# Longformer attention followed by a squared-ReLU feed-forward: inputs through hardware DMA queues with a GpSimd cast, 120-row tiles, a shared PSUM ring and a reordered start

## The chip, the cores and the metric

The kernel runs on one core of one Trainium2 chip. The metric is the device time of one execution in microseconds (us); several executions are timed and their median is given. All runs quoted here count as fast: none took over 1.5% more than the fastest of the same kernel. "PE" is TensorE, "DVE" VectorE, "ACT" ScalarE, "POOL" GpSimd, "SP" the sync engine, which here only issues DMAs. SBUF and PSUM are the on-chip memories; matmul results land in PSUM. A "casting" DMA changes fp32 to fp16 on the way.

## The reference, cut to what matters

```python
def _attn_ref(q, k, v, global_idx):          # q, k, v: (8, 8, 576, 64) float32
    scores = (1 / sqrt(64)) * q @ k.T
    mask = (abs(i - j) <= 32) | is_global[i] | is_global[j]   # 8 global positions
    attn = softmax(where(mask, scores, -1e9))
    return attn @ v

def _moe_ref(x, w_in, w_out):                # x: 4608 x 512, w_in: 512 x 2048, w_out: 2048 x 512
    r = maximum(x @ w_in, 0)
    return (r * r) @ w_out
```

Eight batches of eight heads each give 4,608 tokens of 512 features. The feed-forward (called "expert" below) works on nine chunks of 512 tokens. A chunk can start when the batches that hold its tokens are done.

## The kernel before

The 576 keys of a head lie in five tiles of 116, 116, 116, 116 and 112 rows, with 8 global rows behind them. All inputs come through casting DMAs issued by GpSimd:

```python
KT = 116
KN = (116, 116, 116, 116, 112)
...
    def load_k(b):                            # load_q, load_v alike
        t = knat[b % 2]                       # [128, 5, 512] fp16
        for i in range(NT):
            nc.gpsimd.dma_start(
                out=t[0 : KN[i], i].rearrange("p (h d) -> p h d", d=D),
                in_=k[b, :, KT * i : KT * i + KN[i], :].rearrange("h s d -> s h d"),
            )
        # the global rows follow from a scratch in DRAM, through SP
```

One such DMA moves 116 x 8 runs of 64 numbers. The expert part uses PSUM through two separate tags, two buffers for `ph` and one for `po`:

```python
    def mm1(c, u):
        ph = ps.tile([P, TC], FP32, name="ph", tag="m1", bufs=2)
        ...                                   # 4 matmuls of 512 columns
        nc.scalar.activation(out=rl, in_=ph, func=AF.Relu)
        nc.vector.tensor_tensor(out=gts[c][:, u, :], in0=rl, in1=rl, op=ALU.mult)

    def mm2(c, m, part, tag="m2", bufs=1):
        if part == 0:
            po_now[0] = ps.tile([P, dm], FP32, name="po", tag=tag, bufs=bufs)
        ...                                   # 4 matmuls; after part 3:
            nc.vector.tensor_copy(out=ot, in_=po)      # then a store through SP
```

The main loop has 64 slots, one per head. A slot emits the scores of its head, one transpose for a later head, up to four expert units ("fills", taken from chunk 0 at slot 10, chunk 1 at slot 18 and so on), and the product with v ("PV") of the head before:

```python
    for s in range(B * H):
        b, h = divmod(s, H)
        ...                                   # gathers of global rows at h == 2
        if h == 1 and b >= 1 and b + 1 < B: load_v(b + 1)
        if h == 6 and b + 2 < B: load_k(b + 2); load_q(b + 2)
        et = scores(b, h)
        ...                                   # nb, nhp: a later head pair
        (tr_q if h % 2 == 0 else tr_k)(nb, nhp)
        fill(s, 2)
        if prev is not None: pv(*prev)
        fill(s, 2)
        prev = (b, h, et)
```

The last PV of a batch also copies eight global columns into `xT` on GpSimd (`xT <- gx`), and the expert units of the next chunk wait for that copy. What is left of the fills follows after the loop.

The softmax here doesn't subtract the row's maximum and nothing guards it: scores larger than these inputs give would overflow.

Of the kernel before, what the change touches and what calls it, by code (L numbers as in the profile page):

```python
# [18 lines left out]
KT = 116  # L19
NT = 5  # L20
KN = (116, 116, 116, 116, 112)
# [3 lines left out]
NCOL = 600  # L25

WIN = (
    (0, 0, 0, 0, 156),
    (1, 0, 156, 84, 188),
    (2, 0, 344, 208, 96),  # L30
    (2, 1, 0, 304, 100),
    (3, 1, 100, 332, 188),
    (4, 1, 288, 448, 152),
# [6 lines left out]
def kernel(  # L40
# [37 lines left out]
    for i in range(2):  # L78
        nc.sync.dma_start(
            out=gq64[64 * i : 64 * i + 64],  # L80
            in_=gsrc.to_broadcast((NG, H)).unsqueeze(2),
        )
    gp64 = sbt("gp64", [P, 1], I64)
    nc.vector.memset(gp64.bitcast(I32), 0)
    nc.sync.dma_start(out=gp64[KT : KT + NG, :], in_=gsrc)
    g64 = sbt("g64", [1, NG], I64)
    nc.sync.dma_start(out=g64, in_=global_idx.unsqueeze(0))

# [3 lines left out]
    nc.gpsimd.iota(pidx, pattern=[[0, 4]], base=0, channel_multiplier=1)  # L92
    phead = sbt("phead", [P, 4], I32)
# [7 lines left out]
    icb = sbt("icb", [P, 4], I32)  # L101
    nc.gpsimd.iota(icb, pattern=[[2 * H * S, 4]], base=0, channel_multiplier=0)
# [13 lines left out]

    knat = [sbt(f"knat{i}", [P, NT, H * D], FP16) for i in range(2)]
    qnat = [sbt(f"qnat{i}", [P, NT, H * D], FP16) for i in range(2)]
    vx = [sbt(f"vx{i}", [P, NT, H * P], FP16) for i in range(2)]
    for t in knat:  # L120
        nc.vector.memset(t[96:128], 0.0)
    for t in vx:
        nc.vector.memset(t.rearrange("p t (h x) -> p t h x", x=P)[:, :, :, 64:128], 1.0)
        nc.vector.memset(t[96:128].rearrange("p t (h x) -> p t h x", x=P)[:, :, :, 0:64], 0.0)
    qz = []
    for i in range(2):
        qa = sbt(f"qa{i}", [P, NCOL], FP16)
        qb = sbt(f"qb{i}", [P, NCOL], FP16)
        nc.vector.memset(qa[64:128], 0.0)
        nc.vector.memset(qb[0:64], 0.0)  # L130
        qz.append((qa, qb))


    gscr = {}
    gstv = sbt("gstv", [P, P], FP16)
    nc.gpsimd.memset(gstv[:, 64:128], 1.0)

    def gather(c):
        for nm, src in (("k", k), ("q", q), ("v", v)):
            st = gstv if nm == "v" else sbt("gst", [P, D], FP16, bufs=4)  # L140
            nc.gpsimd.indirect_dma_start(  # L141
                out=st[:, 0:D], out_offset=None,
                in_=src.rearrange("b h s d -> (b h s) d"),
                in_offset=bass.IndirectOffsetOnAxis(ap=gidx[:, c : c + 1], axis=0),
            )
            w = P if nm == "v" else D
            scr = dram.tile([P, w], FP16, name=f"gscr_{nm}{c}")
            nc.sync.dma_start(out=scr, in_=st)
            gscr[(nm, c)] = scr.rearrange("(b g h) d -> b g (h d)", b=2, h=H)


    def load_k(b):
        t = knat[b % 2]
        for i in range(NT):
            nc.gpsimd.dma_start(  # L155
                out=t[0 : KN[i], i].rearrange("p (h d) -> p h d", d=D),
                in_=k[b, :, KT * i : KT * i + KN[i], :].rearrange("h s d -> s h d"),
            )
        scr = gscr[("k", b // 2)][b % 2]
        nc.sync.dma_start(  # L160
            out=t[KT : KT + NG], in_=scr.unsqueeze(1).to_broadcast((NG, NT, H * D))
        )

    def load_q(b):
        t = qnat[b % 2]
        for i in range(NT):
            nc.gpsimd.dma_start(  # L167
                out=t[0 : KN[i], i].rearrange("p (h d) -> p h d", d=D),
                in_=q[b, :, KT * i : KT * i + KN[i], :].rearrange("h s d -> s h d"),
            )  # L170
        scr = gscr[("q", b // 2)][b % 2]
        nc.sync.dma_start(out=t[KN[-1] : KN[-1] + NG, NT - 1], in_=scr)

    def load_v(b):
        t = vx[b % 2]
        for i in range(NT):
            nc.gpsimd.dma_start(  # L177
                out=t[0 : KN[i], i].rearrange("p (h x) -> p h x", x=P)[:, :, 0:D],
                in_=v[b, :, KT * i : KT * i + KN[i], :].rearrange("h s d -> s h d"),
            )  # L180
        scr = gscr[("v", b // 2)][b % 2]
        nc.sync.dma_start(
            out=t[KT : KT + NG], in_=scr.unsqueeze(1).to_broadcast((NG, NT, H * P))
        )

    def load_batch(b):
        load_k(b)
        load_q(b)
        load_v(b)

    w_in = sbt("w_in", [P, NDM, dff], FP16)
    w_out = sbt("w_out", [P, NFF, dm], FP16)

    gather(0)
    load_k(0)
    load_q(0)
# [7 lines left out]

    xT = sbt("xT", [P, NDM, B * S], FP16)
    gts = {}

    def mm1(c, u):
        if c not in gts:
            gts[c] = sbt("gt", [P, NFF, TC], FP16, bufs=2)  # L210
        ph = ps.tile([P, TC], FP32, name="ph", tag="m1", bufs=2)
# [11 lines left out]
    def mm2(c, m, part, tag="m2", bufs=1):  # L223
        if part == 0:
            po_now[0] = ps.tile([P, dm], FP32, name="po", tag=tag, bufs=bufs)
# [6 lines left out]
        if part == 3:  # L232
            ot = sbt("ot", [P, dm], FP32, bufs=3)
# [22 lines left out]
    acc = ps.tile([P, 2, 512], FP32, name="acc", tag="acc")  # L256
    nc.vector.memset(acc, 0.0)

    def tr_q(b, hp):
# [7 lines left out]
        for r, t in zip((slice(0, 64), slice(64, 128)), qz[hp % 2]):  # L267
            nc.vector.tensor_copy(
                out=t[r, 0:456].rearrange("p (g x) -> p g x", x=GRP)[:, :, 0:GTOK],
                in_=pt[r, 0 : 3 * GTOK].rearrange("p (g x) -> p g x", x=GTOK),  # L270
            )
            nc.vector.tensor_copy(out=t[r, 456:600], in_=pt[r, 3 * GTOK : S])
            nc.vector.tensor_copy(
                out=t[r, 0:456].rearrange("p (g x) -> p g x", x=GRP)[:, :, GTOK:GRP],
                in_=pt[r, S : S + NG].unsqueeze(1).to_broadcast((64, 3, NG)),
            )
# [28 lines left out]
    av = acc[:, :, 0:BANKC].rearrange("p b (k x) -> p b k x", x=GRP)  # L305

    def pv(b, h, et):
        v0 = h * P - (64 if h % 2 else 0)
# [14 lines left out]
        rec = sbt("rec", [P, 2, 2, GTOK], FP32, bufs=2)  # L323
# [26 lines left out]
    tr_q(0, 0)  # L350


    g32 = sbt("g32", [1, NG], I32)
    nc.vector.tensor_copy(
        out=g32, in_=g64.bitcast(I32).rearrange("p (g two) -> p g two", two=2)[:, :, 0]
    )
    gpart = sbt("gpart", [P, 1], FP32)
    nc.vector.tensor_copy(out=gpart, in_=gp64.bitcast(I32)[:, 0:1])


    rows = sbt("rows", [P, 3], FP32)
    nc.gpsimd.memset(rows, 1.0)  # L362
    for col, bs, cm in ((0, KT - 1, -1), (1, KN[-1] - 1, -1), (2, -KT, 1)):
        nc.gpsimd.affine_select(
            out=rows[:, col : col + 1], in_=rows[:, col : col + 1],
            compare_op=ALU.is_ge, fill=0.0, base=bs, pattern=[[0, 1]], channel_multiplier=cm,
        )
    nc.gpsimd.affine_select(
        out=rows[:, 2:3], in_=rows[:, 2:3],
        compare_op=ALU.is_ge, fill=0.0, base=KT + NG - 1, pattern=[[0, 1]], channel_multiplier=-1,  # L370
    )

    U0 = 36
    UN = 200
    ub = sbt("ub", [P, UN], FP16)
    nc.gpsimd.memset(ub, 1.0)
    nc.gpsimd.affine_select(
        out=ub, in_=ub, compare_op=ALU.is_ge, fill=0.0,
        base=window + U0, pattern=[[-1, UN]], channel_multiplier=1,
    )  # L380
    nc.gpsimd.affine_select(
        out=ub, in_=ub, compare_op=ALU.is_ge, fill=0.0,
        base=window - U0, pattern=[[1, UN]], channel_multiplier=-1,
    )
    mask = sbt("mask", [P, 2 * SCW], FP16)
    colq = sbt("colq", [P, 2 * SCW], FP32)
    own = sbt("own", [P, 2 * SCW], FP16)
    nc.gpsimd.memset(own, 0.0)
    nc.gpsimd.memset(colq, 0.0)
    for t, bank, so, c0, w in WIN:  # L390
        base = bank * SCW + so
        rv = rows[:, t // 4 : t // 4 + 1]
        for grp in range(4):
            lo, hi = max(grp * GRP, c0), min(grp * GRP + GTOK, c0 + w)
            if lo < hi:
                q0 = lo - 8 * grp
                n = hi - lo
                u = q0 - KT * t + U0
                o = base + lo - c0
                nc.vector.tensor_scalar(  # L400
                    out=mask[:, o : o + n], in0=ub[:, u : u + n], scalar1=rv, scalar2=None,
                    op0=ALU.mult,
                )
                ol, oh = max(q0, KT * t), min(q0 + n, KT * (t + 1))
                if ol < oh:
                    s = slice(o + ol - q0, o + oh - q0)
                    nc.gpsimd.memset(own[:, s], 1.0)
                    nc.gpsimd.iota(
# [30 lines left out]
    for s in range(B * H):  # L439
# [4 lines left out]
        if h == 1 and b >= 1 and b + 1 < B:  # L444
            load_v(b + 1)
# [47 lines left out]
```

## Time and profile before

| | before |
|---|---|
| median of the first three executions | 487.89 us |
| profiled span | 486.7 us |
| PE busy | 340.7 us, 70% |
| first scores, first expert matmul (timeline) | 40.3 us, 141 us |
| exponential of slot 18, of slot 58 (timeline) | 183.2 us, 385.5 us |

The page of the kernel before: busy tenths in 40 slices of 12.2 us, and the DMA queues (packets, MB, time as a share of 16 engines' span).

```profile
span 486.7 us, 6333 instructions
PE   0012153006149989989996998998799898998985
POOL 6781930778684966867667786765730100100000
DMA  1992999999999999999999999999991100101001
...
q0 software_dynamic: 384096, 19.62, 110.7%
q1 hardware_dynamic: 7970, 10.75, 7.7%
```

PE is busy for only a fifth of the first ten slices, while the DMA engines are busy without a break from the fifth slice to the thirtieth. The software queue, the one that GpSimd fills, holds almost all packets: 384,096 for 19.62 MB.

Four stretches of the windows view (us, then busy time of each engine and its instructions, the clock granted to PE, the DMA share and GB/s): to the end of batch 0's heads, to slot 18, to slot 58, to the end.

```profile
core 0: us, PE busy (x) PEld busy (x) DVE busy (x) ACT busy (x) POOL busy (x), PEclk, DMA share, GB/s
0.00:122.00 122.00, 25.42 (x172) 17.92 (x172) 41.66 (x109) 20.92 (x27) 70.33 (x76) 1.00 1.33 69
122.00:183.00 61.00, 41.09 (x272) 23.11 (x273) 29.67 (x79) 27.75 (x42) 43.06 (x40) 1.00 1.59 64
183.00:386.00 203.00, 184.28 (x1330) 105.66 (x1328) 142.57 (x382) 131.49 (x201) 126.16 (x111) 1.00 1.52 74
386.00:487.00 101.00, 89.89 (x470) 42.83 (x468) 42.49 (x99) 41.68 (x68) 1.61 (x8) 0.99 0.09 34
```

The DMA share adds up the times of all packets over 16 engines. A share above 1 (1.33 to 1.59 here, and the 110.7% above) means that records of packets overlap; it is not a rate of use.

Three lines of the waits view (who waited for whom: us in total, times, longest):

```profile
PE ptq L264 <- DMA qnat_92<-in_q_dram: 30.8, 5, 21.5
PE po L228 <- DVE ot L234: 23.1, 26, 1.8
PE ph L213 <- POOL xT L344: 20.6, 3, 15.9
```

Two groups (busy us, mean ns | idle before) and one DMA issue (KB each, median us from issue to landing):

```profile
L219 DVE TENSOR_TENSOR gt<-rl 128x512 f16<-128x512 f16 x144 | 57.5, 421 | 37.5 <-ACT rl L218 36.3
L155 POOL DMA_DIRECT2D knat_90<-in_k_dram x20 | 34.4, 1722 | 37.1 <-issue 23.5
...
knat_89<-in_k_dram POOLq DMA_DIRECT2D x16, 116.0 KB, 11.5
```

A load takes GpSimd 1.72 us to issue in the mean, and a 116-row one lands 11.5 us after its issue (median).

### The profile page before, as it was taken

To read this page: it belongs to the slowest core of one execution; us is meant where nothing else is said; L and a number is where in the kernel's file an instruction comes from. 1 tells how busy PE (TensorE), PEld (TensorE's weight loads), DVE (VectorE), ACT (ScalarE), POOL (GpSimd) and SP (SyncE) were. 2 spreads that over 40 slices of the span, in tenths; PEclk is the share of its full clock that TensorE was granted. 3 is DMA by queue.
4 is the path that set the end of the run, shared out by engine and by line. 5 is a ranking of instruction groups with operands and counts; after the bars stand their busy time and mean duration, and the time that the engine had idled before them with its cause. 6 is when DMAs were issued, how large, how long until landed. Compare 5 with 4: busy or idle time off the path is not lost.

```text
span 486.7 us, 6333 instructions
## 1 busy us (share of the span) xinstructions
PE 340.7 (70%) x2240; PEld 189.5 (39%) x2240; DVE 256.4 (53%) x666; ACT 221.8 (46%) x337; POOL 241.1 (50%) x233
## 2 busy tenths in 40 slices
PE   0012153006149989989996998998799898998985
PEld 0001032004115545545553554554455454443432
DVE  5407145006307658866865766885586685341431
ACT  1001044005118648837844963973694595350520
POOL 6781930778684966867667786765730100100000
PEclk9999999999999999999999999999999999999999
DMA  1992999999999999999999999999991100101001
GB/s 12 61 55 9 37 190 176 52 51 52 56 64 50 44 103 95 45 66 125 58 77 113 48 50 113 84 57 85 96 53 45 44 1 22 67 0 64 23 22 65
DMA packets 392097, 30.77 MB, mean 63 GB/s; under 512 B 384194, under 2 KB 386626, under 8 KB 392066
## 3 DMA queue, kind: packets, MB, share of 16 engines
q0 software_dynamic: 384096, 19.62, 110.7%
q1 hardware_dynamic: 7970, 10.75, 7.7%
q8 instruction: 17, 0.28, 0.2%
q14 instruction: 14, 0.11, 0.1%
HBM read 38.14 MB, written 9.70 MB: 98 GB/s over the span
## 4 chain that ended last, share of the span: by engine, by line
PE 33%; POOL 33%; issue 24%; DVE 5%; DMA 2%; ACT 2%; POOLq 0%; SPq 0%; DVEq 0%
PE ph L213 16%; PE po L228 13%; POOL knat_90 L155 7%; POOL qnat_92 L167 6%; POOL vx_93 L177 5%; POOL qnat_91 L167 4%; POOL knat_89 L155 4%; POOL vx_94 L177 3%; DVE ot L234 2%; DMA qnat_91<-in_q_dram 2%; PE acc L312 2%; POOL xT L344 2%; PE sc L292 1%; POOL gst L141 1%; ACT rec L324 1%
## 5 line engine op out<-in xcount | busy, mean ns | idle before, releaser
L213 PE MATMUL ph<-xT,w_in 128*128 128x512 f16 x576 | 136.3, 384 | 20.6 <-POOL xT L344 20.6
L228 PE MATMUL po<-w_out,gt 128*128 128x512 f16 x576 | 134.3, 379 | 23.2 <-DVE ot L234 23.1
L218 ACT ACTIVATE rl<-ph 128x512 f16<-128x512 f32 x144 | 83.5, 599 | 64.0 <-PE ph L213 63.2
L322 ACT ACTIVATE ln<-acc 64x576 f32<-64x576 f32 x64 | 41.3, 645 | 119.0 <-PE acc L312 118.2
L228 PEld LDWEIGHTS <-gt 128*128 128x128 f16 x576 | 55.0, 97 | 82.4 <-issue 27.6
L213 PEld LDWEIGHTS <-w_in 128*128 128x128 f16 x576 | 55.7, 99 | 78.4 <-issue 23.9
L297 ACT ACTIVATE er<-sc 128x880 f16<-128x880 f32 x64 | 58.0, 907 | 59.2 <-PE sc L292 58.9
L219 DVE TENSOR_TENSOR gt<-rl 128x512 f16<-128x512 f16 x144 | 57.5, 421 | 37.5 <-ACT rl L218 36.3
L329 DVE TENSOR_TENSOR xT<-acc,rec 64x576 f16<-64x576 f32 x64 | 48.3, 755 | 27.1 <-ACT rec L324 26.9
L155 POOL DMA_DIRECT2D knat_90<-in_k_dram x20 | 34.4, 1722 | 37.1 <-issue 23.5
L302 DVE TENSOR_TENSOR et<-er,mask 128x880 f16<-128x880 f16 x64 | 39.5, 617 | 15.8 <-ACT er L297 15.5
L344 POOL COPY xT<-gx 128x4 f16 x64 | 14.5, 227 | 60.9 <-DVE gx L340 57.5
L177 POOL DMA_DIRECT2D vx_93<-in_v_dram x20 | 34.3, 1720 | 20.7 <-DVE mask L425 11.0
L324 ACT ACTIVATE rec<-ln 64x576 f32<-64x576 f32 x64 | 43.6, 681 | 2.0
L167 POOL DMA_DIRECT2D qnat_92<-in_q_dram x20 | 34.3, 1719 | 18.5 <-issue 18.5
L167 POOL DMA_DIRECT2D qnat_91<-in_q_dram x20 | 34.3, 1719 | 18.0 <-issue 18.0
L325 DVE TENSOR_REDUCE gs<-acc 128x8 f32<-128x32 f32 x64 | 12.3, 192 | 55.1 <-ACT ln L322 53.9
L234 DVE COPY ot<-po 128x512 f32<-128x512 f32 x36 | 24.7, 685 | 31.5 <-PE po L228 31.1
L177 POOL DMA_DIRECT2D vx_94<-in_v_dram x20 | 34.3, 1719 | 13.8 <-issue 7.4
L292 PEld LDWEIGHTS <-kT 128*128 128x128 f16 x384 | 30.2, 105 | 16.4 <-DVE kT L284 2.3
L155 POOL DMA_DIRECT2D knat_89<-in_k_dram x20 | 34.7, 1741 | 1.1 <-DMA vx_94<-in_v_dram 0.9
L282 PE MATMUL ptk<-identity,knat_89 128*128 128x128 f16 x80 | 8.1, 241 | 37.5 <-POOL rows L362 31.1
(83 smaller groups left out, 271.5 us busy)
## 6 DMA issues: line engine op xcount, KB each, us to landing
out_dram<-ot SPq DMA_DIRECT2D x36, 256.0 KB
w_in<-in_moe_w_in_dram POOLq DMA_DIRECT2D x1, 2048.0 KB, 19.1
w_out<-in_moe_w_out_dram POOLq DMA_DIRECT2D x1, 2048.0 KB, 28.8
knat_89<-in_k_dram POOLq DMA_DIRECT2D x16, 116.0 KB, 11.5
qnat_91<-in_q_dram POOLq DMA_DIRECT2D x16, 116.0 KB, 13.2
vx_93<-in_v_dram POOLq DMA_DIRECT2D x16, 116.0 KB, 12.0
knat_90<-in_k_dram POOLq DMA_DIRECT2D x16, 116.0 KB, 12.6
qnat_92<-in_q_dram POOLq DMA_DIRECT2D x16, 116.0 KB, 14.9
```

What stands on the lines that cost most here:

```text
L155: nc.gpsimd.dma_start(out=t[0 : KN[i], i].rearrange("p (h d) -> p h d", d=D), in_=k[b, :, KT * i : KT * i + KN[i], :].rearrange("h s d -> ...
L167: nc.gpsimd.dma_start(out=t[0 : KN[i], i].rearrange("p (h d) -> p h d", d=D), in_=q[b, :, KT * i : KT * i + KN[i], :].rearrange("h s d -> ...
L177: nc.gpsimd.dma_start(out=t[0 : KN[i], i].rearrange("p (h x) -> p h x", x=P)[:, :, 0:D], in_=v[b, :, KT * i : KT * i + KN[i], :].rearrange ...
L213: nc.tensor.matmul(ph, w_in[:, t, u * P : (u + 1) * P], xT[:, t, c * TC : (c + 1) * TC], start=(t == 0), stop=(t == NDM - 1),)
L218: nc.scalar.activation(out=rl, in_=ph, func=AF.Relu)
L219: nc.vector.tensor_tensor(out=gts[c][:, u, :], in0=rl, in1=rl, op=ALU.mult)
L228: nc.tensor.matmul(po, gts[c][:, f, m * P : (m + 1) * P], w_out[:, f, :], start=(f == 0), stop=(f == NFF - 1),)
L297: nc.scalar.activation(out=er.rearrange("p (b c) -> p b c", b=2), in_=sc[:, :, 0:SCW], func=AF.Exp, bias=0.0, scale=scale,)
L302: nc.vector.tensor_tensor(out=et, in0=er, in1=mask, op=ALU.mult)
L322: nc.scalar.activation(out=ln[nr], in_=av[dr, :, :, 0:GTOK], func=AF.Ln)
L324: nc.scalar.activation(out=rec[nr], in_=ln[nr], func=AF.Exp, scale=-1.0)
L329: nc.vector.tensor_tensor(out=xT[nr, hp, b * S : (b + 1) * S].rearrange("p (b k x) -> p b k x", b=2, k=2), in0=av[nr, :, :, 0:GTOK], in1=r ...
```

## The change

The intent was to take the loads off GpSimd's slow casting path: hardware queues (SP, ACT) bring fp32 into a staging tile, and an engine casts it. Batch 0 comes in two head halves so that work starts early; 16 expert units run while batch 1 is being cast; PSUM is pooled (`ph` and `po` take turns in one ring of three buffers); and the tiles get 120 rows. The core of the diff (mask building, global-row handling, buffer counts and the order of small set-up work are cut):

```diff
-KT = 116
-KN = (116, 116, 116, 116, 112)
+KT = 120
+KN = (120, 120, 120, 120, 96)
...                                            # WIN, NCOL and the q copies follow the new tiles
+    def fetch(eng, src, b, st=None, hs=slice(0, H)):
+        if st is None:
+            st = sbt("stg", [P, NT, H * D], FP32, bufs=3)
+        for i in range(NT):
+            eng.dma_start(
+                out=st[0 : KN[i], i].rearrange("p (h d) -> p h d", d=D)[:, hs],
+                in_=src[b, hs, KT * i : KT * i + KN[i], :].rearrange("h s d -> s h d"),
+            )
+        return st
+    def cast(op, dst, st, hs=slice(0, H), w=D):
+        for t, n in ((slice(0, 4), KT), (slice(4, 5), KN[4])):
+            op(out=dst[0:n, t]..., in_=st[0:n, t]...)
+    st0k = fetch(nc.sync, k, 0, None, h03)     # then st0q on ACT, st0v; later heads 4 to 7
...
-        ph = ps.tile([P, TC], FP32, name="ph", tag="m1", bufs=2)
+        ph = ps.tile([P, TC], FP32, name="ph", tag="m", bufs=3)
-            po_now[0] = ps.tile([P, dm], FP32, name="po", tag=tag, bufs=bufs)
+            po_now[0] = ps.tile([P, dm], FP32, name="po", tag="m", bufs=3)
...
+        if h == 1 and 0 < b < B - 1:
+            cast(nc.gpsimd.tensor_copy, knat[n % 2], sts["k"])
+            gload_kq(n)
+        if h == 2 and 0 < b < B - 1:
+            cast(nc.gpsimd.tensor_copy, qnat[n % 2], sts["q"])
+        if h == 4 and 0 < b < B - 1:
+            cast(nc.gpsimd.tensor_copy, vx[n % 2], sts["v"], w=P)
+            gload_v(n)
+        if h == 5 and b + 2 < B and b > 0:
+            fetch_next(n + 1)
+        if s == H:
+            pv(*prev)
+            prev = None
+            fill(2 * H, 4)
+            cast(nc.gpsimd.tensor_copy, knat[1], sts["k"])
+            cast(nc.gpsimd.tensor_copy, qnat[1], sts["q"])
+            fill(2 * H, 8)
+            tr_k(1, 0)
+            fill(2 * H, 2)
+            tr_q(1, 0)
+            cast(nc.gpsimd.tensor_copy, vx[1], sts["v"], w=P)
+            fill(2 * H, 2)
+            fetch_next(2)
```

## The prediction

> **What bounds the kernel now.** Two regimes. (a) Until about 183 us it is bound by loading. The windows view gives PE only 27 us of busy time in the first 122 us. The timeline shows the first scores at 40.3 us, the first PV finished at 65 us, a stall of PE from 81 to 101 us on batch 1's q (waits: PE ptq on DMA qnat_92, 30.8 us), and the first expert matmul at 141 us (waits: PE ph on POOL xT, 15.9 us: global-column copies stand behind DMA issues on GpSimd). Expert chunk 1 starts at 183.3. (b) After that PE, with ACT close behind, sets the pace: a head with four mm1 fills takes 4.575 us, but a chunk (eight heads) takes 40.5 us on average (183.3 to 385.7 for five), not 8 x 4.575 = 36.6, because mm2 has one PSUM buffer: PE po waits for DVE ot 23.1 us in all, about 0.77 us per output tile in the tail.
>
> **Loading.** A batch is 13,824 rows. The casting loads write 128-byte packets of 32 ns (median in the packet records) plus small 4-byte ones: about 48 us per batch, DMA over 90% busy from 85 to 377 us. They keep GpSimd busy 26 us per batch. Hardware-queue packets take 18 ns at 256 B, 48 ns at 1 KB. My estimate for a 256-byte fp32 batch is 864 packets per DMA engine, 16 to 26 us. The Trainium skill (DMA: Bandwidth & Descriptors, "SWDGE vs HWDGE vs iDMA") says a cast in a DMA needs the GpSimd path; the trace agrees, all casting loads are in the software queue. The cast moves: GpSimd memsets here take about 0.95 ns per element, so I estimate 2.8 us per tensor, 8.4 us per batch.
>
> **What it is worth.**
> 1. Start: first scores at about 22 us instead of 40; PV at about 28; eight heads at 3.2 us end at about 54; 16 expert units (about 0.87 us each) run while batch 1 is cast; batch 1's first scores at about 72 us instead of 115; chunk 1 (slot 18) at about 110 us instead of 183. Gain about 73 us.
> 2. Pooled PSUM ring of three (m): chunk period 36.5 to 38 us instead of 40.5, tail 6 us shorter. Gain about 20 to 25 us.
> 3. Loss: GpSimd casts against DVE. The Trainium skill (SBUF — State Buffer, "Who interferes with whom") says a VectorE instruction with two SBUF inputs contends with a GpSimd instruction that reads SBUF; this trace has none long enough to show it. DVE is about 70% busy, so I allow 1 us of PE per cast pair, about 10 us in all. Output stores queued behind fetches: 0 to 10 us.
>
> Sum: 488 - 73 - 22 + 10 = 403 us. Range 380 to 435. Chances: faster by over 2% 0.94, within 2% 0.03, slower 0.03.
>
> **What shows it right or wrong.** Timeline: times of first scores, first expert matmul, chunk 1. DMA view: software queue nearly only weights; DMA share well under 0.9. Waits: PE po on DVE ot nearly gone. Groups: GpSimd casts of 128x2048 about 2.2 us. Longer DVE gt and et show the lock.
>
> **What would make it wrong.** Hardware rows of 256 B at over 40 ns, so that loading stays the bound; output stores stuck behind fetches, stopping DVE through the two output buffers; casts far slower than 1 ns per element; the gather chain coming late.

## The result, and the profile after

The new kernel takes 400.65 us (median of 4; 399.53 to 403.49) against 488.61 us before. The ratio is 0.8202, 95% interval 0.8144 to 0.8261. Here and below a ratio is the mean time of one kernel's fast runs over that of the kernel before in the same rounds, so it is not quite the ratio of the medians. The result is correct.

The page of the new kernel, same lines (slices of 10.0 us):

```profile
span 401.8 us, 6380 instructions
PE   0037529779768999899989989998999999999996
POOL 5929427250048006200930180036001001000000
DMA  8979998961999942991599189410001002001002
...
q1 hardware_dynamic: 117618, 38.29, 52.3%
q0 software_dynamic: 5904, 4.39, 7.0%
```

PE now starts in the third slice, and the DMA engines rest between loads after the start. The hardware queue carries the inputs; the software queue has little but the weights.

The same four stretches of the windows view:

```profile
0.00:78.00 78.00, 36.32 (x216) 22.33 (x216) 49.00 (x106) 31.15 (x45) 43.88 (x73) 1.00 1.04 176
78.00:118.00 40.00, 30.47 (x235) 19.47 (x235) 27.75 (x64) 21.48 (x29) 7.49 (x13) 0.85 0.79 140
118.00:309.00 191.00, 181.33 (x1322) 103.67 (x1321) 158.50 (x340) 130.91 (x201) 54.90 (x76) 1.00 0.64 110
309.00:402.00 93.00, 88.26 (x471) 42.60 (x468) 42.30 (x95) 41.76 (x68) 1.61 (x8) 1.00 0.10 37
```

The clock granted to PE was 0.85 in the second stretch, against 1.00 there before; what that cost was not separated.

By the exponentials of slots 18 and 58 in the two timelines, the span of 84.9 us that was saved splits into 65.7 us before slot 18 (183.2 to 117.5), 11.2 us from slot 18 to 58 (202.3 to 191.1 us of work), and 8.0 us after slot 58 (101.2 to 93.2). DVE grew busier in the third stretch, although it has no new work there: 143 us of 203 before, 158 us of 191 now.

The waits view of the new kernel has no line of PE `po` waiting for DVE `ot` any more. In their place are these:

```profile
PE acc L403 <- DVE xT L420: 17.6, 15, 2.2
ACT rl L312 <- DVE gt L313: 12.4, 11, 2.1
PE ph L307 <- POOL xT L435: 5.6, 1, 5.6
```

Two groups of the new kernel, split by shape, answer to those of before:

```profile
L313 DVE TENSOR_TENSOR gt<-rl 128x512 f16<-128x512 f16 x144 | 81.9, 592 | 24.2 <-ACT rl L312 23.0
L105 POOL CAST knat_70<-stg 120x2048 f16<-120x2048 f32 x4 | 7.6, 1889 | 0.0
```

`gt`, whose code did not change, went from 421 to 592 ns in the mean. A GpSimd cast of 2,048 elements per partition takes 1.89 us. The fp32 load of a 120-row k tile lands in 5.0 us (issues of the page; 11.7 us for q, 6.1 us for v; the trace records a landing for only 9 of these 84 loads of k, q and v):

```profile
stg<-in_k_dram SPq DMA_DIRECT2D x28, 240.0 KB, 5.0
```

### The profile page after: what moved, and what is told of

It is laid out like the page before. It is cut to its first block, busy times and chain, and to the rows that moved or that the text cites. A ratio compares the mean times of both kernels' runs of the same rounds, so it can differ in the third digit from the quotient of the medians.

```text
span 401.8 us, 6380 instructions
## 1 busy us (share of the span) xinstructions
PE 336.4 (84%) x2240; PEld 188.1 (47%) x2240; DVE 277.5 (69%) x603; ACT 225.3 (56%) x341; POOL 107.9 (27%) x169
## 4 chain that ended last, share of the span: by engine, by line
PE 72%; DVE 18%; ACT 5%; issue 2%; POOL 1%; DMA 1%; POOLq 0%; DVEq 0%
PE po L322 31%; PE ph L307 26%; DVE gt L313 6%; PE acc L403 6%; PE sc L383 5%; DVE xT L420 3%; DVE et L393 2%; PE ptq L356 2%; PE ptk L373 1%; ACT ln L415 1%; ACT ln L413 1%; ACT er L388 1%; DMA gp_100<-in_global_idx_dram 1%; ACT rl L312 1%; DVE knat_69 L105 1%
## 5 line engine op out<-in xcount | busy, mean ns | idle before, releaser
L313 DVE TENSOR_TENSOR gt<-rl 128x512 f16<-128x512 f16 x144 | 81.9, 592 | 24.2 <-ACT rl L312 23.0
L420 DVE TENSOR_TENSOR xT<-acc,ln 64x576 f16<-64x576 f32 x64 | 48.3, 754 | 22.5 <-ACT ln L415 22.1
L393 DVE TENSOR_TENSOR et<-er,mask 128x880 f16<-128x880 f16 x64 | 42.3, 662 | 15.0 <-ACT er L388 14.3
L415 ACT ACTIVATE ln<-ln 64x576 f32<-64x576 f32 x64 | 43.6, 681 | 2.0
L403 PE MATMUL acc<-et,vx_73 128*128 128x160 f16 (+2 forms) x192 | 20.3, 251 | 12.6 <-DVE xT L420 12.6
L403 PEld LDWEIGHTS <-vx_73 128*128 128x128 f16 x192 | 15.8, 109 | 20.1 <-issue 7.8
L403 PE MATMUL acc<-et,vx_74 128*128 128x160 f16 (+2 forms) x192 | 18.0, 232 | 5.0 <-DVE xT L420 5.0
L403 PEld LDWEIGHTS <-vx_74 128*128 128x128 f16 x192 | 14.2, 100 | 12.9 <-DVE xT L420 4.8
L373 PEld LDWEIGHTS <-knat_69 128*128 128x128 f16 x80 | 5.6, 106 | 29.2 <-DVE knat_69 L105 20.0
L375 DVE COPY kT<-ptk 128x640 f16<-128x640 f16 x32 | 15.7, 489 | 1.0 <-PE ptk L373 0.4
## 6 DMA issues: line engine op xcount, KB each, us to landing
stg<-in_q_dram SPq DMA_DIRECT2D x28, 240.0 KB, 11.7
```

The source lines that it names most:

```text
L393: nc.vector.tensor_tensor(out=et, in0=er, in1=mask, op=ALU.mult)
L403: nc.tensor.matmul(acc[:, bank, o : o + w], vx[b % 2][:, t, v0 : v0 + P], et[:, base : base + w], start=(i % 3 == 0), stop=(i % 3 == 2), s ...
L415: nc.scalar.activation(out=rec[nr], in_=ln[nr], func=AF.Exp, scale=-1.0)
L420: nc.vector.tensor_tensor(out=xT[nr, hp, b * S : (b + 1) * S].rearrange("p (b k x) -> p b k x", b=2, k=2), in0=av[nr, :, :, 0:GTOK], in1=r ...
```

## The experiments

Twelve kernels were run, each timed against the kernel before over three rounds. All were correct except `a2_nocast`.

| run | kernel | median us | ratio |
|---|---|---|---|
| (result) | the new kernel | 400.65 | 0.8202 |
| a1_split | new, PSUM split as before | 424.12 | 0.8650 |
| b1_ring | before, shared PSUM ring | 478.30 | 0.9744 |
| a2_nocast | new, no casts from batch 2 on (wrong result) | 389.54 | 0.7943 |
| a3_sw | new, casting loads from batch 2 on | 389.29 | 0.7946 |
| b2_120 | before, 120-row tiles | 425.55 | 0.8687 |
| b3_120ring | before, 120-row tiles and ring | 395.62 | 0.8094 |
| a8_116 | new, 116-row tiles | 544.97 | 1.1134 |
| a4_noahead | new, no expert units ahead | 401.04 | 0.8195 |
| a5_whole | new, batch 0 loaded whole | 408.94 | 0.8353 |
| a6_pieces | new, casts in pieces | 390.72 | 0.7995 |
| c1_best | a combination, below | 375.72 | 0.7677 |
| c2_best | the same, improved | 370.77 | 0.7607 |

Differences between kernels of different rounds are taken from their ratios: a step of 0.01 is 4.9 us.

### a1_split and b1_ring: what the PSUM ring is worth

```diff
# a1_split: the new kernel          # b1_ring makes the opposite edit in the kernel before
-        ph = ps.tile([P, TC], FP32, name="ph", tag="m", bufs=3)
+        ph = ps.tile([P, TC], FP32, name="ph", tag="m1", bufs=2)
-            po_now[0] = ps.tile([P, dm], FP32, name="po", tag="m", bufs=3)
+            po_now[0] = ps.tile([P, dm], FP32, name="po", tag="m2", bufs=1)
```

> The new kernel with the old split of PSUM (two buffers for ph, one for po). Theory: the shared ring of three removes the waits of PE po for DVE ot (23.1 us in the kernel before, none after) and is worth most of them in all stages: 415 to 424 us, waits of PE po for DVE ot back at about 20 us. Rival: in the steady stage ACT and the GpSimd casts hold PE anyway, so only the tail (10 output tiles at 0.7 us) pays: 406 to 410 us.

> The kernel before with nothing but the shared ring of three PSUM buffers. Theory (PE bounds its steady stage): 465 to 470 us, all 23 us of waits gone. Rival (its steady stage is also held by the casting loads, which need about 43 to 48 us per batch against 40.5): only the tail pays, 478 to 483 us, and slots 18 to 58 keep about 5.0 us per head.

Without the ring the new kernel takes 0.8650 instead of 0.8202: the ring is worth 21.9 us in it, as the theory said (424.12 us is at the upper end of its range). The waits of `po` for `ot` are back at 21.9 us.

In the kernel before, the same ring brings only 0.9744 (interval 0.9674 to 0.9813, so it is not clear that it passes 2%), about 12.5 us. Its heads of slots 18 to 58 still take 5.11 us each, as against 5.06 without the ring, although no wait of `po` for `ot` is left. This is the rival's case. Another wait took the place of the one removed, in the stretch from 183 to 385 us of b1_ring:

```profile
PE ph L213 <- POOL xT L344: 15.1, 4, 5.0
```

The same wait came to 4.7 us there in the kernel before. That line is the copy of the global columns on GpSimd, which stands behind DMA issues. So loading seems to have been a limit in the steady stage too, just under the limit that PSUM set; b3_120ring below tests it.

### a2_nocast and a3_sw: the steady stage

```diff
# a2_nocast: the new kernel, casts of batches 2 to 7 left out
-            cast(nc.gpsimd.tensor_copy, knat[n % 2], sts["k"])     # also those of qnat and vx
# a3_sw: the new kernel, batches 2 to 7 loaded by casting DMAs again
+    def sload(dst, src, n, w=D):
+        for i in range(NT):
+            nc.gpsimd.dma_start(
+                out=dst[0 : KN[i], i].rearrange("p (h x) -> p h x", x=w)[:, :, 0:D],
+                in_=src[n, :, KT * i : KT * i + KN[i], :].rearrange("h s d -> s h d"),
+            )
# k and q of batch b + 2 at h == 6 (batch 2: at slot 8), v of batch b + 1 at h == 1; fetch_next and the casts go
```

> The new kernel with the GpSimd casts of batches 2 to 7 left out (wrong result on purpose; loads stay). Theory: the casts hold VectorE through the shared port: gt returns from a mean of 592 ns to about 450 ns, heads of slots 18 to 58 go from 4.78 us to about 4.5 us, total 386 to 392 us. Rival (the lost time per head comes from ACT or from the PE order, not from casts): within 3 us of the new kernel, 398 to 403 us.

> The new kernel with batches 2 to 7 loaded by casting DMAs from GpSimd again, without casts; start, ring and run-ahead as in the new kernel. Theory: casting loads take about 45 us per batch, more than the 38 us that a batch then takes, so the steady stage becomes bound by loading: 420 to 440 us, DMA busy over 90% to about slot 56. Rival: loads hide behind PE in the steady stage and the gain was all in the start: 390 to 402 us, even faster because no cast holds VectorE.

The "shared port" of the expectation stands for the contention that the prediction allowed for; a6_pieces below tests it. Without the casts the new kernel loses 12.7 us (0.7943), and its heads of slots 18 to 58 take 4.535 us instead of 4.778. So the casts cost what the theory said, and their effect is not hidden.

a3_sw was the surprise. The theory behind the prediction said that casting loads cannot keep up. With them the kernel is as fast as with no cast at all (0.7946), the heads again take 4.535 us, and PE is busy without a gap in the steady stage. The hardware queues and the GpSimd cast do not pay from batch 2 on: they lose 12.5 us against the path that they replaced. The theory fell.

The trace showed why to doubt it. The casting loads of k in a3_sw were issued in 0.90 us each and landed in 4.3 us; in the kernel before it was 1.94 us and 11.5 us (medians). The code of the DMA was the same, except that its tile had 120 rows instead of 116.

### b2_120 and b3_120ring: the tile height alone

The packet records of the trace, counted by size, show the difference. Each casting load should write 128-byte packets, one per row and head (called rows below). There is a second kind of packet, of 4 bytes:

| kernel | casting queue, 128-byte packets | 4-byte packets | time of all its 4-byte packets over 16 engines |
|---|---|---|---|
| before (116 rows) | 112,128 | 269,408 | 246 us |
| b2_120 (120 rows) | 112,128 | 8,288 | 5 us |

The Trainium skill (DMA: Bandwidth & Descriptors, "Why a DMA increments its semaphore by 16 and not by 1") says that a DMA is shared among k of the 16 DMA engines, k being the largest number up to 16 that divides the outer sizes of both sides. 116 = 4 x 29 gives k = 4, 120 gives 15, 112 and 96 give 16. Four engines would then take 232 packets each of a 116-row load (928 / 4), and twelve would have none. The counts fit exactly if each idle engine gets as many 4-byte packets as a working one gets rows. The 96 loads of 116 rows would carry 96 x 12 x 232 = 267,264 of them, and 2,144 are left over for all else, which is 16 for each of the queue's 134 DMAs (120 loads, 12 gathers, 2 weight loads). The 96 loads of 120 rows (64 per engine, one idle engine) would carry 96 x 64 = 6,144, and 8,288 - 6,144 leaves the same 2,144. a3_sw agrees: its 72 loads of 120 rows and 107 DMAs give 72 x 64 + 107 x 16 = 6,320, and 6,320 were counted. The packet records kept here name no engine, so the split over engines is inferred from the counts; what the 4-byte packets do is not in the trace. An exception that the same section reports, k = 16 for some direct copies issued from GpSimd, does not fit the count of the 116-row loads.

The kernel before held a control that had not been read: its 24 loads of 112 rows were issued in 0.83 us each, its 96 loads of 116 rows in 1.94 us or more. The issues of the k loads there, then in b2_120 (ns, minimum/median/maximum; the minimum of the first two lines is the 112-row tile):

```profile
L155 POOL DMA_DIRECT2D knat_89<-in_k_dram x20: 828/1939/2024, 8.4 to 287.9; - x20
L155 POOL DMA_DIRECT2D knat_90<-in_k_dram x20: 828/1939/1968, 58.5 to 328.7; - x20
L155 POOL DMA_DIRECT2D knat<-in_k_dram x40: 792/930/1012, 8.4 to 263.4; - x40
```

```diff
# b2_120: the kernel before
-KT = 116
-KN = (116, 116, 116, 116, 112)
-NCOL = 600
+KT = 120
+KN = (120, 120, 120, 120, 96)
+NCOL = 608
...                     # WIN, U0, UN and the copies of q as in the new kernel
# b3_120ring: b2_120 with tag="m", bufs=3 for ph and po
```

> The kernel before with nothing but 120-row tiles (and the window tables and the query copy that go with them); loads still cast in the DMA from GpSimd, PSUM still split. Theory, from the run with casting loads in the steady stage: the slow loads of the kernel before come from the 116-row shape, whose DMAs carry about 2,200 extra 4-byte packets each. With 120 rows the 4-byte packets almost vanish (from 269,408 to under 15,000), a load's issue takes 0.9 us instead of 1.94, chunk 1 starts near 150 us instead of 183, total 440 to 460 us. Rival (the casting path is slow as such and only looked fast because it was less crowded): 482 to 490 us.

> The kernel before with 120-row tiles and the shared ring of three PSUM buffers. Theory: with loading off the limit the ring gains its full 20 to 25 us on top (heads of slots 18 to 58 at 4.53 us, as in the run with casting loads): 415 to 438 us. Rival (the gains only add as measured alone, 11 us for the ring): 10 to 13 us under the run with 120 rows alone.

The page of b2_120 (slices of 10.6 us; queue; one issue line):

```profile
span 425.9 us, 6269 instructions
DMA  1929999994929987391929198955011001001011
q0 software_dynamic: 122976, 18.58, 65.9%
...
knat<-in_k_dram POOLq DMA_DIRECT2D x32, 120.0 KB, 4.3
```

Four rows more per tile, with the mask tables and query copies that go with them, take the kernel before from 488 to 425.55 us, better than the theory's 440 to 460: the slot-18 exponential comes at 127.6 us, not at 150. The companion edits cannot explain it: PE's busy time goes from 340.7 to 339.9 us and VectorE's from 256.4 to 251.8, but GpSimd's, which issues the loads, from 241.1 to 141.1. Whether the shorter issues or the missing packets count for more was not separated. With the ring as well it is 395.62 us. The ring is worth 29 us here (0.8687 to 0.8094), against 12.5 us in the kernel before and 20 to 25 expected: with loading off the limit, its full gain shows. (The expected range of the total, 415 to 438 us, was missed, since b2_120 had already come out lower than expected.) The windows of b3_120ring, cut as before at the ends of batch 0's heads, slot 18 and slot 58:

```profile
0.00:76.00 76.00, 22.44 (x151) 15.84 (x152) 36.66 (x85) 18.09 (x24) 43.93 (x77) 1.00 1.39 110
76.00:121.00 45.00, 42.08 (x300) 24.69 (x298) 33.25 (x84) 30.40 (x47) 22.78 (x39) 1.00 1.21 88
121.00:301.00 180.00, 180.00 (x1327) 104.14 (x1325) 139.50 (x342) 131.56 (x201) 72.67 (x111) 1.00 0.84 77
301.00:394.00 93.00, 88.14 (x470) 42.65 (x468) 42.17 (x95) 41.65 (x68) 1.62 (x8) 1.00 0.10 37
```

In its third stretch PE is busy the whole time. This kernel has casting loads from GpSimd, no cast, no halves, no units ahead, and it is 5 us faster than the new kernel (0.8094 against 0.8202; the intervals do not overlap).

### a8_116: does the shape matter to hardware queues?

```diff
# the new kernel
-KT = 120
-KN = (120, 120, 120, 120, 96)
+KT = 116
+KN = (116, 116, 116, 116, 112)
...                     # WIN, U0, UN, the copies of q and one cleared acc tile as in the kernel before
```

> The new kernel with 116-row tiles again (tables of the kernel before, one cleared acc tile as there); hardware queues and GpSimd casts as in the new kernel. Theory that the 116-row shape hurts the casting path alone: 398 to 406 us. Rival that it hurts every load (fewer DMA engines share a DMA of 116 rows): batch loads take over 38 us, 415 to 480 us, and the DMA of a 116-row tile lands later than one of 112 rows.

It matters more. The kernel takes 544.97 us, slower than the kernel before, and the rival's range was too kind. Page of a8_116, DMA slices and the chain of waits by line:

```profile
DMA  2442995343334334434333433343332011010202
...
SPq L97 61%; PE ph L311 10%; PE po L326 10%; DMA stg<-in_v_dram 4%; DMA out_dram<-ot 2%; PE acc L410 1%; PE sc L388 1%; DVE ot L332 1%; SPq L190 1%; DVE xT L427 1%; DVE et L398 0%; POOL vx L105 0%; SPq L334 0%; PE ptq L360 0%; DVE kT L380 0%
```

The DMA engines are at 0.3 to 0.4 of their time in the middle of the run, and yet the chain runs for 61% of the span through the issue of these loads on SP. The records agree with k again, if a hardware-queue DMA ends with one 4-byte packet on each engine that it used. The new kernel has 108 loads of 120 rows where a8_116 has 108 of 116 rows, so it should have 108 x (15 - 4) = 1,188 more such packets; it has 3,037 against 1,849, which is 1,188. One packet of 256 B took 18.4 ns in the mean here; with 12 x 232 + 3 x 56 = 2,952 of them on the busiest engines, a batch needs about 54 us (an estimate from these numbers), and batches of loads began every 45 to 51 us from batch 2 on. That fits a pace set by the engine share and not by the byte rate. It is not shown to be that alone: issuing a full-height load of all heads took SP 3.2 us in the median, 1.2 us in the new kernel. The trace records no landings of these loads, so the rival's last point stays open. The hardware queues alone, without the new tile height, would have been a loss.

### a4_noahead and a5_whole: the other two parts of the start

```diff
# a4_noahead: the new kernel, the four fill(2 * H, ...) calls at s == H removed
# a5_whole: the new kernel
-    st0k = fetch(nc.sync, k, 0, None, h03)
+    st0k = fetch(nc.sync, k, 0)               # q, v alike; second fetches and second casts removed
```

> The new kernel without the 16 expert units ahead of batch 1's scores (they go into slots 10 to 17 instead). What the prediction assumed (they fill time in which PE would only wait): 408 to 416 us. Rival (batch 1's data is there at about 66 us, so the block of 17 us delays the scores of batch 1 by about 10 us, and the same units in slots 14 to 17 cost only 1.3 us per head): 392 to 399 us.

> The new kernel with batch 0 loaded and cast whole instead of in two head halves. Theory: the first scores come later (23.5 us now, 27 to 33 us then) and everything behind shifts with them: 404 to 410 us. Rival: batch 1's scores wait for batch 1's data and for the expert block in any case, so a later first head is hidden: 398 to 403 us.

a4_noahead is at 0.8195, the new kernel at 0.8202: the units ahead are worth nothing that these runs can tell. Without them the first exponential of batch 1 comes at 74.1 us instead of 78.1, and that of slot 18 at 117.0 instead of 117.5. What the block brings forward, it pays back by holding up batch 1. Neither the prediction's range nor the rival's was met; the time lies between them. One thing was not separated: without the units, PE's granted clock is 1.00 from 74 to 117 us, while it was 0.85 from 78 to 118 us in the new kernel.

a5_whole is at 0.8353, which is 7.4 us slower, and its first exponential comes at 31.9 us instead of 23.5. Slot 18 moves by 6.4 us. So the halves do pay, and a later first head is not hidden.

### a6_pieces: how the casts hold VectorE

The Trainium skill (SBUF — State Buffer, "Who interferes with whom") says that a VectorE instruction with two SBUF inputs contends with a GpSimd instruction that reads SBUF, and that the loser waits for the whole instruction. `gt = rl * rl` is such an instruction. The timeline of the new kernel shows it beside two casts made during batch 4's heads (start us, us, what; lines between left out):

```profile
195.74 0.60 ACT L312 ACTIVATE rl<-ph 128x512 f16<-128x512 f32 x1 [0.22 <-PE ph L307]
196.60 2.44 POOL L105 CAST qnat_72<-stg 120x2048 f16<-120x2048 f32 x2
197.22 4.69 DVE L313 TENSOR_TENSOR gt<-rl 128x512 f16<-128x512 f16 x2
198.99 2.64 POOL L105 CAST vx_74<-stg 120x2048 f16<-120x2048 f32 x2
201.25 0.60 ACT L312 ACTIVATE rl<-ph 128x512 f16<-128x512 f32 x1 [2.06 <-DVE gt L313]
```

The two `gt` took 4.69 us instead of 0.86. They began inside the first cast, ran on past its end at 199.0 us, and ended near the end of the second at 201.6 us. ACT waited 2.06 us for `gt` in between. The direct test makes the casts' instructions short:

```diff
# the new kernel
-        for t, n in ((slice(0, 4), KT), (slice(4, 5), KN[4])):
+        for t, n in [(slice(i, i + 1), KN[i]) for i in range(NT)]:
```

> The new kernel with each GpSimd cast cut into five instructions of one row tile (512 elements) instead of two. If VectorE gets the shared port between GpSimd instructions, the longest gt falls from 3.95 us to about 1 us and the total to 391 to 397 us (the run without casts: 389.5). Rival: GpSimd instructions that follow one another without a gap keep VectorE out as long as the series lasts: longest gt still 2.5 us or more, 398 to 405 us.

The durations of `gt` in ns (minimum/median/maximum, start of first and last), first in the new kernel, then in a6_pieces:

```profile
L313 DVE TENSOR_TENSOR gt<-rl x144: 405/425/3946, 62.3 to 384.6; 128x512 f16<-128x512 f16 x144
```

```profile
L313 DVE TENSOR_TENSOR gt<-rl x144: 402/425/861, 62.6 to 371.6; 128x512 f16<-128x512 f16 x144
```

The longest `gt` falls from 3.95 to 0.86 us, and the kernel to 390.72 us (0.7995), within 2.5 us of the run with no casts. The same bytes are cast on the same engine, and the casts even take more of its time in all (77.9 us against 60.4); only the time for which one instruction holds on is shorter. This supports the lock, and it speaks against a plain lack of VectorE time. One thing is beyond the page: 3.95 us is longer than any one cast instruction (2.16 us at most), and the `gt` above lasted through parts of three of them, so with long casts VectorE lost its turn more than once in a row. Why it does so beside long casts and not beside short ones is not shown.

### c1_best and c2_best: a version that beats both

c1_best is a3_sw with a new start: no block of units ahead; batch 1's loads and casts put before the weights; the weights issued only after batch 1's k and q are cast; the two tiny index loads put before batch 0's. c2_best cuts the remaining casts into pieces as in a6_pieces and moves the filling of batch 1's v padding (and the load of its global v rows) behind its k and q casts.

```diff
# c1_best, against a3_sw (core)
+            sts["k"] = fetch(nc.sync, k, 1)
+            sts["q"] = fetch(nc.sync, q, 1)
+            gload_kq(1)
+            sts["v"] = fetch(nc.sync, v, 1)
+            cast(nc.gpsimd.tensor_copy, knat[1], sts["k"])
+            cast(nc.gpsimd.tensor_copy, qnat[1], sts["q"])
             for i in range(4):
                 nc.gpsimd.dma_start(out=w_in[:, :, ts(i, 512)], in_=wv[:, :, ts(i, 512)])
+            cast(nc.gpsimd.tensor_copy, vx[1], sts["v"], w=P)
-        if s == H:                             # the special block is gone, fills start at slot 10
# c2_best, against c1_best
-        for t, n in ((slice(0, 4), KT), (slice(4, 5), KN[4])):
+        for t, n in [(slice(i, i + 1), KN[i]) for i in range(NT)]:
-            pads(1, nc.gpsimd)                 # from ahead of fetch k, 1
+            pads(1, nc.gpsimd)                 # to just ahead of the cast of vx[1]
```

> A version meant to be the best: casting loads from GpSimd in 120-row tiles from batch 2 on (as in the run at 389.3 us), no expert block ahead of batch 1, batch 1's loads and casts ahead of the weights, the two small index loads ahead of batch 0. Theory: batch 1's data is there before batch 0 ends, so its first scores come at about 57 us instead of 77, chunk 1 at about 100 us instead of 115, first scores of all at about 20 us: 371 to 379 us. Rival: the weights now land too late and PE waits for them instead: 384 to 392 us.

> The version of 375.7 us with each remaining cast (batches 0 and 1) cut into pieces of one row tile and the filling of batch 1's v padding moved behind the casts of its k and q, out of the way of VectorE's cast of batch 0's second half (4.26 us there, 1.24 us when nothing holds it). Theory: head 2 of batch 0 starts at about 32 us instead of 35.9 and all that follows moves by 3 to 4 us: 371 to 373 us. Rival (the hold merely moves to another VectorE instruction): 375 to 377 us.

c1_best takes 375.72 us and c2_best 370.77 us (0.7607). In c1_best the first exponential of batch 1 comes at 56.4 us and that of slot 18 at 101.7 us; in c2_best at 49.5 and 94.6 us. The exponential of head 2 of batch 0 moves from 35.9 to 31.2 us, as the theory of c2_best said. Which of the edits of c1_best and c2_best brings how much was not separated. The windows of c2_best, cut at the same events as before:

```profile
0.00:50.00 50.00, 18.32 (x151) 14.58 (x152) 35.20 (x92) 21.37 (x34) 41.20 (x75) 0.90 0.88 181
50.00:95.00 45.00, 42.49 (x300) 24.98 (x300) 33.38 (x84) 30.56 (x47) 30.51 (x46) 0.88 1.91 151
95.00:274.00 179.00, 179.00 (x1318) 103.56 (x1316) 138.59 (x340) 130.63 (x200) 72.27 (x111) 1.00 0.83 78
274.00:367.00 93.00, 88.75 (x477) 43.03 (x474) 42.81 (x96) 42.19 (x68) 1.62 (x8) 1.00 0.10 37
```

From slot 18 to 58 PE has no gap. Most of its idle time, 31.7 us, lies in the first 50 us. The granted clock was 0.90 and 0.88 in the first two stretches; its cost was not separated.

## Why the prediction was right or wrong

**The time and the range: right.** 403 us was predicted, 400.65 us measured.

**The start (73 us): right in size, but mostly for another reason.** First scores 22 predicted, 22.5 measured; PV 28 against 31.2; batch 1's first scores 72 against 77.5; slot 18 at 110 against 117.5. The gain was 65.7 us. But b2_120, with none of the moves that the prediction listed, has slot 18 at 127.6 us, which is 55.6 of the 65.7; and a8_116, with all of them and 116 rows, has it at 182.9 us, where the kernel before has it at 183.2.

**The PSUM ring (20 to 25 us): right.** 21.9 us in the new kernel (a1_split), 8.1 us of it in the tail after slot 58 (6 were predicted). It was not seen that its worth depends on the loads: 12.5 us in the kernel before, 29 us once the tiles had 120 rows.

**The loss to the casts (10 us): right.** 12.7 us (a2_nocast), through the interference named (a6_pieces). Output stores stuck behind fetches, allowed 0 to 10 us, do not show in the new kernel; in a8_116 DVE did wait 85.7 us for output stores to free a buffer.

**The cause of the slow loads: wrong.** The step that failed, in the prediction's words: "The casting loads write 128-byte packets of 32 ns (median in the packet records) plus small 4-byte ones: about 48 us per batch". The 4-byte packets had been seen, but they were taken for a property of the casting path. They belong to the 116-row shape, at 3 per row. With 120 rows the casting path has 0.07 per row or so and keeps up with PE (a3_sw, b3_120ring). The 48 us were also too many for the kernel before, whose batches of k loads began every 38 to 42 us from batch 2 on. So the hardware queues got the credit for what four more rows per tile did: 64 us alone (b2_120). The prediction listed the tile height nowhere. a8_116 shows that the queues without the height are worse than the kernel before, and b3_120ring that height and ring without the queues are better than the new kernel. The sum came out because the new kernel contains the true cause too. That was luck.

**The units ahead of batch 1: counted as part of the start's gain, but worth nothing measurable** (a4_noahead).

**The rate of hardware-queue packets: right.** The estimate was 16 to 26 us per batch. Packets of 256 B took 26.1 ns in the mean; with 12 x 64 + 3 x 48 = 912 per batch on the busiest engines that makes 23.8 us.

## What to carry to other kernels

Before a load is moved to another queue, look at the row count of its outermost dimension: by the packet counts, 116 rows went through 4 of 16 DMA engines and 120 through 15, and that outweighed every other part of this change. Compare, in one profile, the issues of tiles of different height. When a change bundles several edits, run each alone and together with the others, as their worth depends on which limit stands above them. Casts on GpSimd beside two-input VectorE work should be cut into short instructions, or left to the DMA.

## What the Trainium skill lacked or had wrong

- DMA: Bandwidth & Descriptors: it states how k is chosen, and the counts here agree for both kinds of queue, but it lacks what the casting path does with the engines left out. The counts fit one 4-byte packet per row of a working engine on each of them: 267,264 such packets in the kernel before (9 ns in the median, 14.6 in the mean, of all 4-byte packets of the queue), 6,144 with 120 rows. Its exception (k = 16 for some copies on that path) was not met in the 116-row loads.
- DMA: Bandwidth & Descriptors: its rule of thumb that hardware queues are generally faster held per packet (26.1 ns for 256 B read in the new kernel against 35.9 ns in b2_120 for the same row cast to 128 B), but the kernel with casting loads (a3_sw) was 12.5 us faster, as much as leaving the casts out (12.7 us).
- SBUF — State Buffer: the contention of a two-input VectorE instruction with GpSimd reads agrees. It lacks that VectorE can lose several turns in a row: `gt` of 0.42 us took 3.95 us beside casts of at most 2.16 us each, and at most 0.86 us beside casts in pieces.
- GPSIMD Engine Reference, "Engine selection": one-input work at roughly line rate fits: 1.89 us for 2,048 elements, 0.92 ns each. No part of the page gives what such work costs the VectorE beside it in time, 12.7 us here.
